# One visit of the divided array per chunk in a fused attention and feed-forward kernel

## The chip, the cores and the metric

The kernel runs on one core of a Trainium2 chip. The time is device microseconds (us) of that core for one execution. Five engines work side by side, each through its own list of instructions in order: TensorE (PE in the profile; its weight loads are PEld), VectorE (DVE), ScalarE (ACT), GpSimd (POOL) and SyncE (SP), which issues the transfers. They meet only through semaphores.

## The reference

Four batches, eight heads, 768 positions, 64 elements a head. Each query sees the 31 keys around it and, besides, 24 summaries of its head: the maximum of the keys and the mean of the values over blocks of 32. The attention's output, 3072 tokens of 512, goes through a feed-forward block with a squared relu.

```python
k_sum = k.reshape(B, H, nb, 32, D).max(axis=3)
v_sum = v.reshape(B, H, nb, 32, D).mean(axis=3)
scores_l = scale * q @ k.T                     # kept where abs(i - j) < 16
scores_s = scale * einsum('bhsd,bhnd->bhsn', q, k_sum) + log(32)
a = softmax(concatenate([scores_l masked, scores_s]))
x = a @ concatenate([v, v_sum])                # to (3072, 512)
r = maximum(x @ w_in, 0)                       # 512 -> 2048
out = (s * r * r + b) @ w_out                  # 2048 -> 512
```

Everything is float32.

## The kernel before

**Chunks, units and blocks.** The 3072 tokens are worked in twelve chunks `c` of 256 tokens, three to a batch. A chunk's attention is four units `p`, each one pair of heads. A unit has four stretches of 64 queries, and each stretch sees a window of 96 keys and the 24 summaries, 120 columns (`KR`). Its feed-forward part is sixteen blocks `f` of 128 hidden elements.

**A unit's way.** `load_unit` brings queries and key windows (tile `qk`), and `load_values` the value windows (`vw`). `fill_k` (L250) and `fill_v` (L255) copy the summaries into both, on POOL from chunk 2 on. `scores` (L285) multiplies 64x64 pieces: two heads and two stretches of queries use the four quarters of the array. `masked` (L306, DVE) adds the mask, scales, and finds the row's extreme. `exps` (L319, ACT) makes exponentials and sums, and `normalize` (L326 to L329, DVE) divides. `transposes` (L342, PE) turns the probabilities into a bank (`pt`), and `turned` (L349, ACT) copies them out (`pT`). `values` (L367) multiplies them by the value windows, in two halves of 64 columns of the array. From chunk 2 on two units share one output bank (`pav`), and `attended` (L377 on ACT, L379 on DVE) splits it into a rounded part `xh` and a rest `xl`, for both units at once.

**A block's way.** From chunk 1 on a product of float32 matrices is three products of rounded parts. `hidden` (L396) does twelve matmuls a block, two blocks to a bank (`ph`, two banks). `activate` does relu and square on ACT (L403, L404), scale and shift on POOL (`g`, L414), and the split into `gh` and `gl` on DVE (L416, L418), each in eight buffers. `project` (L433) does six matmuls a block into two banks (`po`), and `evict` (L441) copies these out after the sixteenth block.

**The order.** The whole order of work is written out as a plan. `at(step, order, fn, ...)` puts a piece of work at a step; step `16 * c + f` belongs to block `f` of chunk `c`. Steps run in order, within a step by the class (`LOAD, SPLIT, ATT, WEIGHTS, HID, PE_ATT, CHAIN, PROJ, EVICT`), within a class as entered. Every engine gets its instructions in this one order. From chunk 3 on the blocks go by fours: `hidden` of four blocks at steps 0, 4, 8 and 12 of a chunk (48 matmuls), their `activate` at their own steps in class `CHAIN`, and `project` of four blocks at steps 3, 7, 11 and 15 (24 matmuls), three steps and one hidden stretch behind: blocks 8 to 11 are projected at step 15.

A unit's attention is placed around the plan by `base`, the step of its scores, and nine `lags`. From chunk 4's third unit on (`by_fours`) units 0 and 1 of chunk `c` have their scores at step 14 of chunk `c - 2`, and units 2 and 3 eight steps later, at step 6 of chunk `c - 1`; values follow eight steps after the scores. So at each of these two steps PE does the values of two units and the scores of two others in one go, a **visit** of the divided array, before it returns to full 128x128 matmuls. Between visits stand two groups of transposes, at steps 3 and 11.

```python
base, v_at = NF * (c - 1) - 2 + 8 * (p // 2), 3 * (p % 2)
if by_fours(c, p):
    lags = (1, 1, 1, 2, 6, 5, 6, 8, 9)
m, e0, e1, n, fv, tr, tu, va, xa = (base + lag for lag in lags)
```

**Banks.** The eight banks of PSUM are two for `po`, two for `ph`, two for scores (`ps_s`, one a head, units 2k and 2k + 1 side by side), one for `pt` (`ps_t`) and one for `pav` (`ps_v`), which also takes the odd units' transposes.

**SP's queue.** It holds every transfer in the plan's order: `qk` and `vw` of each unit, the keys and values of a batch for the summaries (`load_k`, `load_v`, in four `stage` buffers that the output tiles of `evict` share), the small copies of `v_mean`, and the output's stores.

Of the kernel before, what the change touches and what calls it, by code (L numbers as in the profile page):

```python
# [10 lines left out]
F32 = mybir.dt.float32  # L11
F32R = mybir.dt.float32r
# [6 lines left out]
P = 128  # L19
# [7 lines left out]
KR = WIN + NB  # L27
NSUB = 4
T = NSUB * SUB
# [5 lines left out]
NF = DFF // P  # L35
# [9 lines left out]
def windowed_attention_then_relu2_ffn(ctx, tc, qk, vwin, kt, vt, kq, vrow, wp, sb, out):  # L45
# [8 lines left out]
    p2 = ctx.enter_context(tc.tile_pool(name="p2", bufs=2))  # L54
# [36 lines left out]
    def at(step, order, fn, *args):  # L91
        plan[step].append((order, len(plan[step]), fn, args))
# [167 lines left out]
    def scores_of_maxima(p):  # L260
        q, _ = qk_t[0, p]
        for i in range(NSUB):
            for e in range(2):
                r = slice(64 * e, 64 * e + 64)
                o = ps_of[0, p][e][64 * (i % 2) : 64 * (i % 2) + 64, i // 2]
                nc.tensor.matmul(o[:, WIN:], q[r, i * SUB : (i + 1) * SUB], ksum[0, p][r], start=True, stop=True)

    def scores(c, p, j):
        q, kw = qk_t[c, p]
        if j == 0:  # L270
            if c == 0 and p % 2:
                both = [ps_h.tile([P, 2, T], F32, name="ps", tag="ph") for _ in range(2)]
                ps_of[c, p] = [t[:, 0, : 2 * KR].rearrange("p (j k) -> p j k", k=KR) for t in both]
            elif c < 2:
                ps_of[c, p] = [ps_s.tile([P, 4, KR], F32, name="ps", tag="ps") for _ in range(2)]
            elif p % 2 == 0:
                both = [ps_s.tile([P, 4, KR], F32, name="ps", tag="ps") for _ in range(2)]
                ps_of[c, p], ps_of[c, p + 1] = [t[:, :2] for t in both], [t[:, 2:] for t in both]
        for e in range(2):
            r = slice(64 * e, 64 * e + 64)  # L280
            for a in range(2):
                i = 2 * j + a
                o, qi = ps_of[c, p][e][64 * a : 64 * a + 64, j], q[r, i * SUB : (i + 1) * SUB]
                if c > 1:
                    nc.tensor.matmul(o, qi, kw[r, i, :], start=True, stop=True)  # L285
                    continue
                w = win_start(i)
                near = kraw[0, p][r, w : w + WIN] if c == 0 else kw[r, i, :WIN]
                nc.tensor.matmul(o[:, :WIN], qi, near, start=True, stop=True)
                if c == 1:  # L290
                    nc.tensor.matmul(o[:, WIN:], qi, ksum[0, p][r], start=True, stop=True)

    def masked(c, p, j):
        _, ci = place(c)
        if j == 0 and c == 0:
            t = stage.tile([P, 4 * KR + 8], F32, name="pr0", tag="stage")
            pr_of[c, p] = t[:, : 4 * KR].rearrange("p (n k) -> p n k", k=KR)
            mn_of[c, p], sm_of[c, p] = t[:, 4 * KR : 4 * KR + 4], t[:, 4 * KR + 4 :]
        elif j == 0:
            t = p2.tile([P, 4 * KR + 16], F32, name="pr")  # L300
            pr_of[c, p] = t[:, : 4 * KR].rearrange("p (n k) -> p n k", k=KR)
            mn_of[c, p] = p2.tile([P, 4], F32, name="mn")
            sm_of[c, p] = p2.tile([P, 4], F32, name="sums")
        for e in range(2):
            n = 2 * e + j
            nc.vector.tensor_tensor_reduce(  # L306
                out=pr_of[c, p][:, n, :], in0=ps_of[c, p][e][:, j, :], in1=mask_of(NSUB * ci + 2 * j),
                scale=-1.0 / math.sqrt(D), scalar=3.0e38, op0=ALU.add, op1=ALU.min,
                accum_out=mn_of[c, p][:, n : n + 1],
            )  # L310
        if j == 1:
            ps_of.pop((c, p))
            qk_t.pop((c, p))
# [14 lines left out]
        pr = pr_of[c, p]  # L328
        nc.vector.tensor_tensor(pr, pr, rs.unsqueeze(2).to_broadcast([P, 4, KR]), ALU.mult)  # L329

    def by_fours(c, p):

        return (c, p) > (4, 1)

    def transposes(c, p):
        pr = pr_of.pop((c, p))
        if by_fours(c, p) and p % 2:
            pt_of[c, p] = ps_v.tile([P, 4 * P], F32, name="pt", tag="pav")
        else:
            pt_of[c, p] = ps_t.tile([P, 4 * P], F32, name="pt")  # L340
        for n in range(4):
            nc.tensor.transpose(pt_of[c, p][:KR, n * P : (n + 1) * P], pr[:, n, :], ident)  # L342

    def turned(c, p):
        if c == 0 and p > 1:
            pT_of[c, p] = slots.tile([KR, 4 * P], F32, name="pT0", tag="slot")
        else:
            pT_of[c, p] = p2.tile([KR, 4 * P], F32, name="pT")
        nc.scalar.copy(pT_of[c, p], pt_of.pop((c, p))[:KR])  # L349

    def values(c, p):
        vw, pT = vw_t.pop((c, p)), pT_of.pop((c, p))
        if c == 0 and p % 2:
            o_of[c, p] = ps_po.tile([P, DM], F32, name="pav", tag="po")
        elif c < 2 or p % 2 == 0:
            o_of[c, p] = ps_v.tile([P, 2 * T], F32, name="pav")
            if c > 1:
                o_of[c, p + 1] = o_of[c, p][:, T:]
        o = o_of[c, p]
        for i in range(NSUB):  # L360
            for e in range(2):
                oi, pi = o[64 * e : 64 * e + 64, i * SUB : (i + 1) * SUB], pT[:, e * T + i * SUB : e * T + (i + 1) * SUB]
                if c == 1:
                    nc.tensor.matmul(oi, vw[0:WIN, e, i, :], pi[0:WIN], start=True, stop=False)
                    nc.tensor.matmul(oi, vsum[0][0:KR, 2 * p + e], pi, start=False, stop=True)
                else:
                    nc.tensor.matmul(oi, vw[:, e, i, :], pi, start=True, stop=True)  # L367
# [32 lines left out]
    def activate(c, f):  # L400
        ph = ph_of.pop((c, f))
        r = p2.tile([P, T], F32, name="r")
        nc.scalar.activation(r, ph, AF.Relu)  # L403
        nc.scalar.activation(r, r, AF.Square)  # L404
        if c == 0:
            g = p2.tile([P, T], F32, name="g0", tag="gh", bufs=8)
            if f < 1:
                nc.vector.tensor_scalar(g, r, s_col, b_col, ALU.mult, ALU.add)
            else:
                nc.scalar.activation(g, r, AF.Identity, bias=b_col, scale=s_col)  # L410
            gg[c, f] = (g,)
            return
        g = p2.tile([P, T], F32, name="g")
        nc.gpsimd.tensor_scalar(g, r, s_col, b_col, ALU.mult, ALU.add)  # L414
        gh = p2.tile([P, T], F32R, name="gh", tag="gh", bufs=8)
        nc.vector.tensor_copy(gh, g)  # L416
        gl = p2.tile([P, T], F32R, name="gl", bufs=8)
        nc.vector.tensor_tensor(gl, g, gh.bitcast(F32), ALU.subtract)  # L418
        gg[c, f] = gh, gl

# [23 lines left out]
            nc.sync.dma_start(out[r0 : r0 + P, :], o)  # L444


    LOAD, SPLIT, ATT, WEIGHTS, HID, PE_ATT, CHAIN, PROJ, EVICT = range(9)


    FIRST, FIRST_SCALED, FIRST_TURNED = -100, 8, 2  # L450
# [31 lines left out]
    for c in range(1, NC):  # L482
        bi, ci = place(c)
        for p in range(NPAIR):
            if c == 1:

                base, v_at = [0,3,6,8][p], 0
                lags = (1, 2, 2, 3, 4, 4, 5, 6, 7)
            else:

                base, v_at = NF * (c - 1) - 2 + 8 * (p // 2), 3 * (p % 2)
                lags = ((1, 2, 2, 3, 6, 4, 5, 8, 9), (2, 3, 4, 5, 6, 6, 7, 8, 9))[p % 2]
                if by_fours(c, p):
                    lags = (1, 1, 1, 2, 6, 5, 6, 8, 9)
            m, e0, e1, n, fv, tr, tu, va, xa = (base + lag for lag in lags)
            if ci == 0:
                at(base - 7, LOAD, load_k, bi, p)
                at(base - 2, ATT, k_max, bi, p)
                if p < 2:
                    for third in range(3):  # L500
                        at(base + v_at - 5 + third, LOAD, load_v, bi, p, third)
                        at(base + v_at - 1 + third // 2, ATT, v_sum, bi, p, third)
                    at(base + v_at + 1, ATT, v_mean, bi, p)
            if (c, p) not in ((1, 0),):
                at(base - 6, LOAD, load_unit, c, p)
            at(base + v_at, LOAD, load_values, c, p)
            if c > 1:
                at(base - (2 if by_fours(c, p) else 1), ATT, fill_k, c, p)
            for j in range(2):
                at(base, PE_ATT, scores, c, p, j)  # L510
                at(m, ATT, masked, c, p, j)
                at((e0, e1)[j], ATT, exps, c, p, j)
            at(n, ATT, normalize, c, p)
            if c > 1:
                at(fv, ATT, fill_v, c, p)
            at(tr, PE_ATT, transposes, c, p)
            at(*((tr, CHAIN) if by_fours(c, p) else (tu, ATT)), turned, c, p)
            at(va, PE_ATT, values, c, p)
            if c < 2 or p % 2 == 0:
                at(xa, ATT, attended, c, p)  # L520
    for f in range(NF):
# [9 lines left out]
    for i in range(NC * NF):  # L531
        c, f = divmod(i, NF)
# [67 lines left out]
```

## Time and profile before

| | |
|---|---|
| time, median of 3 runs | 646.78 us (646.62 to 647.96) |
| the profiled execution, its own time | 646.86 us |
| its span, first to last instruction | 645.2 us |
| PE busy | 634.1 us, 98% |
| DVE, ACT, POOL busy | 332.4, 333.5, 155.6 us |

The span is that of the one profiled execution. Busy time of PE is modelled at the ends of matmuls, so it says little on how well the array is used. In a row of a timeline the columns are the start and the duration in us, the engine, the line of the kernel, the operation, output and inputs, shapes, and a count where instructions of one kind are drawn together; brackets at the end give idle time ahead of it and what ended it. The chain of work that ended last gives start, duration, engine, tile, line and count.

### The profile page before, as it was taken

The numbers are of one execution on the slowest core, as the hardware profiler recorded it, in microseconds if no ns is written. First come the engines' busy times: TensorE is split into PE (matmuls) and PEld (weight loads), VectorE is DVE, ScalarE is ACT, GpSimd is POOL, SyncE is SP. The second block draws the span as 40 slices with busy tenths as digits, with TensorE's granted clock in tenths as the row PEclk, the third lists the DMA queues.
The fourth block names the chain that finished last, engine by engine and source line by source line (L and its number), as shares of the span: only waits on it lengthen the run. The fifth ranks groups of instructions, "written<-read, shape, count | busy, mean of one in ns | idle before, by whom it ended". The sixth has DMA issues, their size and how long they took to land.

```text
span 645.2 us, 14148 instructions
## 1 busy us (share of the span) xinstructions
PE 634.1 (98%) x5316; PEld 554.8 (86%) x5316; DVE 332.4 (52%) x1076; ACT 333.5 (52%) x987; POOL 155.6 (24%) x325
## 2 busy tenths in 40 slices
PE   8799999999999999999999999999999999999997
PEld 6566668999989889989988998998899899899896
DVE  6897968885443533565433434347435334332311
ACT  5899997844445543534535434435535435443321
POOL 3000004143133223223233132131332232321211
PEclk9899999999999999999999999999999999999999
DMA  9999505045203202433400500513600500100000
GB/s 320 377 383 350 154 1 187 2 105 189 73 2 105 73 2 63 124 102 108 157 2 1 177 2 1 186 34 100 233 2 2 175 3 1 58 2 1 34 2 33
DMA packets 25606, 63.26 MB, mean 98 GB/s; under 512 B 3969, under 2 KB 3969, under 8 KB 25537
## 3 DMA queue, kind: packets, MB, share of 16 engines
q1 hardware_dynamic: 25536, 62.36, 29.3%
q8 instruction: 42, 0.69, 0.5%
q14 instruction: 28, 0.22, 0.1%
HBM read 55.90 MB, written 6.29 MB: 96 GB/s over the span
## 4 chain that ended last, share of the span: by engine, by line
PE 86%; ACT 8%; DMA 4%; SPq 0%; issue 0%
PE po L433 39%; PE ph L396 38%; PE pav L367 3%; PE ps L285 3%; DMA wraw<-in_wp_dram 3%; PE pt L342 3%; ACT wraw L118 2%; ACT wraw L119 2%; DMA vn<-in_vrow_dram 2%; ACT g L410 1%; ACT pr L319 1%; ACT r L404 1%; ACT r L403 1%; SPq L231 0%; ACT pT L349 0%
## 5 line engine op out<-in xcount | busy, mean ns | idle before, releaser
L414 POOL TENSOR_SCALAR g<-r,sb_col 128x256 f32<-128x256 f32 x176 | 102.2, 581 | 406.2 <-ACT r L404 349.5
L416 DVE CAST gh<-g 128x256 fp32r<-128x256 f32 x176 | 52.5, 298 | 274.1 <-POOL g L414 256.0
L403 ACT ACTIVATE r<-ph 128x256 f32<-128x256 f32 x192 | 72.3, 377 | 214.9 <-PE ph L396 214.9
L433 PE MATMUL po<-wh,gl 128*128 128x512 f32 x352 | 141.7, 402 | 0.0
L433 PE MATMUL po<-wh,gh 128*128 128x512 f32 x352 | 138.5, 393 | 0.0
L433 PE MATMUL po<-wl_out,gh 128*128 128x512 f32 x352 | 137.5, 391 | 0.0
L396 PE MATMUL ph<-xh,wl_in 128*128 128x256 f32 x704 | 110.3, 279 | 0.0
L396 PE MATMUL ph<-xl,wh 128*128 128x256 f32 x704 | 108.6, 276 | 0.0
L396 PE MATMUL ph<-xh,wh 128*128 128x256 f32 x704 | 108.6, 276 | 0.0
L396 PEld LDWEIGHTS ph<-xh,wl_in 128*128 128x128 f32 x704 | 97.1, 188 | 5.1 <-ACT r L404 0.5
L396 PEld LDWEIGHTS ph<-xl,wh 128*128 128x128 f32 x704 | 93.4, 188 | 0.0
L396 PEld LDWEIGHTS ph<-xh,wh 128*128 128x128 f32 x704 | 92.9, 188 | 0.0
L418 DVE TENSOR_TENSOR gl<-g,gh 128x256 fp32r<-128x256 f32 x176 | 85.1, 483 | 6.0
L404 ACT ACTIVATE r<-r 128x256 f32<-128x256 f32 x192 | 80.2, 418 | 6.1
L319 ACT ACTIVATE pr<-pr,mn 128x120 f32<-128x120 f32 x176 | 67.2, 383 | 24.7 <-DVE mn L306 24.7
L433 PEld LDWEIGHTS po<-wh,gl 128*128 128x128 f32 x352 | 66.1, 188 | 15.2 <-issue 1.6
L433 PEld LDWEIGHTS po<-wh,gh 128*128 128x128 f32 x352 | 66.1, 188 | 14.2
L433 PEld LDWEIGHTS po<-wl_out,gh 128*128 128x128 f32 x352 | 66.2, 188 | 13.0
L255 POOL COPY vw<-vsum 24x256 f32<-24x256 f32 x80 | 37.5, 509 | 1.3
L396 PEld LDWEIGHTS ph<-x,wf_in 128*128 128x128 f32 x128 | 25.7, 204 | 12.0 <-ACT r L403 3.4
L396 PE MATMUL ph<-x,wf_in 128*128 128x256 f32 x128 | 33.2, 406 | 1.6 <-ACT r L403 1.0
L329 DVE TENSOR_TENSOR pr<-pr,rs 128x480 f32<-128x480 f32 x48 | 32.3, 672 | 1.7
(82 smaller groups left out, 619.9 us busy)
## 6 DMA issues: line engine op xcount, KB each, us to landing
wraw<-in_wp_dram SPq DMA_DIRECT2D x32, 512.0 KB, 9.8
qk<-in_qk_dram SPq DMA_DIRECT2D x44, 368.0 KB, 4.6
vw<-in_vwin_dram SPq DMA_DIRECT2D x48, 192.0 KB, 6.5
out_dram<-o SPq DMA_DIRECT2D x24, 256.0 KB, 2.1
kraw<-in_kt_dram SPq DMA_DIRECT2D x12, 384.0 KB, 4.5
vraw<-in_vt_dram SPq DMA_DIRECT2D x12, 252.0 KB, 3.7
kq<-in_kq_dram SPq DMA_DIRECT2D x4, 512.0 KB, 4.1
vraw<-in_vt_dram SPq DMA_DIRECT2D x6, 264.0 KB
```

Source lines behind the costliest of these rows:

```text
L255: filler(c).tensor_copy(vw_t[c, p][WIN:KR, e], vsum[bi][WIN : WIN + NB, 2 * p + e, :].unsqueeze(1).to_broadcast([NB, NSUB, D]),)
L285: nc.tensor.matmul(o, qi, kw[r, i, :], start=True, stop=True)
L319: nc.scalar.activation(pr, pr, AF.Exp, bias=mn_of[c, p][:, n : n + 1], scale=-1.0, accum_out=sm_of[c, p][:, n : n + 1])
L329: nc.vector.tensor_tensor(pr, pr, rs.unsqueeze(2).to_broadcast([P, 4, KR]), ALU.mult)
L342: nc.tensor.transpose(pt_of[c, p][:KR, n * P : (n + 1) * P], pr[:, n, :], ident)
L396: nc.tensor.matmul(ph, w[:, kc * P : (kc + 1) * P], x[:, kc], start=(n == 0), stop=(n == len(terms) - 1))
L403: nc.scalar.activation(r, ph, AF.Relu)
L404: nc.scalar.activation(r, r, AF.Square)
L414: nc.gpsimd.tensor_scalar(g, r, s_col, b_col, ALU.mult, ALU.add)
L416: nc.vector.tensor_copy(gh, g)
L418: nc.vector.tensor_tensor(gl, g, gh.bitcast(F32), ALU.subtract)
L433: nc.tensor.matmul(po[t], a[:, t * P : (t + 1) * P], w, start=(f == 0 and n == 0), stop=(f == NF - 1 and n == len(terms) - 1),)
```

## The change

From chunk 4 on (`together(c)`, in place of `by_fours`) all four units of a chunk have the same `base`, step 15 of chunk `c - 2`. At that step PE does `values` of all four units of chunk `c - 1` and then `scores` of all four units of chunk `c`, in a new class `VISIT` behind `CHAIN` and ahead of `PROJ`. Chunk 4's scores join the values of the last two units of chunk 3, which stand one step ahead of them. Transposes of units 0 and 1 move to step 7 and those of 2 and 3 stay at step 11; between them and the visit are four steps or more.

Scores of units 2 and 3 go to the two `ph` banks, and their values to the bank of `pt`. Units 2 and 3 are masked and exponentiated first (`ATT`), units 0 and 1 behind them (`NEXT`), all in the step after the visit and ahead of that step's hidden blocks. `pr`, `mn`, `sums` and `pT` get four buffers in place of two, and `gl` seven in place of eight. Loads, fills and reductions move to steps that fit.

```diff
+    def together(c):
+        return c >= 4
     def scores(c, p, j):
...
+            elif p == 2 and together(c):
+                both = [ps_h.tile([P, 2 * T], F32, name="ps", tag="ph")[:, : 4 * KR] for _ in range(2)]
+                both = [t.rearrange("p (n k) -> p n k", k=KR) for t in both]
+                ps_of[c, p], ps_of[c, p + 1] = [t[:, :2] for t in both], [t[:, 2:] for t in both]
...
-            t = p2.tile([P, 4 * KR + 16], F32, name="pr")
+            t = p2.tile([P, 4 * KR + 16], F32, name="pr", bufs=4)
...
-            mn_of[c, p] = p2.tile([P, 4], F32, name="mn")
-            sm_of[c, p] = p2.tile([P, 4], F32, name="sums")
+            mn_of[c, p] = p2.tile([P, 4], F32, name="mn", bufs=4)
+            sm_of[c, p] = p2.tile([P, 4], F32, name="sums", bufs=4)
...
-        if by_fours(c, p) and p % 2:
+        if together(c) and p % 2:
             pt_of[c, p] = ps_v.tile([P, 4 * P], F32, name="pt", tag="pav")
...
-            pT_of[c, p] = p2.tile([KR, 4 * P], F32, name="pT")
+            pT_of[c, p] = p2.tile([KR, 4 * P], F32, name="pT", bufs=4)
...
-            o_of[c, p] = ps_v.tile([P, 2 * T], F32, name="pav")
+            if together(c) and p:
+                o_of[c, p] = ps_t.tile([P, 2 * T], F32, name="pav", tag="pt")
+            else:
+                o_of[c, p] = ps_v.tile([P, 2 * T], F32, name="pav")
...
-        gl = p2.tile([P, T], F32R, name="gl", bufs=8)
+        gl = p2.tile([P, T], F32R, name="gl", bufs=7)
...
-    LOAD, SPLIT, ATT, WEIGHTS, HID, PE_ATT, CHAIN, PROJ, EVICT = range(9)
+    LOAD, SPLIT, ATT, NEXT, WEIGHTS, HID, PE_ATT, CHAIN, VISIT, PROJ, EVICT = range(11)
...
-                if by_fours(c, p):
-                    lags = (1, 1, 1, 2, 6, 5, 6, 8, 9)
+                if together(c):
+                    base, v_at = NF * (c - 1) - 1, (9, 10, 4, 5)[p]
+                    tr = 8 + 4 * (p // 2)
+                    lags = (1, 1, 1, 2, (12, 13, 11, 11)[p], tr, tr, 16, 17)
...
-                at(base - 7, LOAD, load_k, bi, p)
-                at(base - 2, ATT, k_max, bi, p)
+                at(base - (12 - p if together(c) else 7), LOAD, load_k, bi, p)
+                at(base - (7 - p if together(c) else 2), ATT, k_max, bi, p)
...
-                at(base - (2 if by_fours(c, p) else 1), ATT, fill_k, c, p)
+                at(base - (2 if together(c) else 1), ATT, fill_k, c, p)
...
-                at(base, PE_ATT, scores, c, p, j)
-                at(m, ATT, masked, c, p, j)
-                at((e0, e1)[j], ATT, exps, c, p, j)
+                at(base, VISIT if together(c) else PE_ATT, scores, c, p, j)
+                at(m, NEXT if together(c) and p < 2 else ATT, masked, c, p, j)
+                at((e0, e1)[j], NEXT if together(c) and p < 2 else ATT, exps, c, p, j)
...
-            at(*((tr, CHAIN) if by_fours(c, p) else (tu, ATT)), turned, c, p)
-            at(va, PE_ATT, values, c, p)
+            at(*((tr, CHAIN) if together(c) else (tu, ATT)), turned, c, p)
+            at(va, VISIT if together(c) else PE_ATT, values, c, p)
```

More of the change, by code (lines that the diff above doesn't have):

```diff
@@ L329, in normalize @@
         nc.vector.tensor_tensor(pr, pr, rs.unsqueeze(2).to_broadcast([P, 4, KR]), ALU.mult)
-    def by_fours(c, p):
-        return (c, p) > (4, 1)
     def transposes(c, p):
         pr = pr_of.pop((c, p))
-        if by_fours(c, p) and p % 2:
+        if together(c) and p % 2:
             pt_of[c, p] = ps_v.tile([P, 4 * P], F32, name="pt", tag="pav")
```

## The prediction

> **What bounds the kernel now.** I read the page's shares first, then the chain that ended last.
>
> ```profile
> span 645.2 us, 14148 instructions
> PE 634.1 (98%) x5316; PEld 554.8 (86%) x5316; DVE 332.4 (52%) x1076; ACT 333.5 (52%) x987; POOL 155.6 (24%) x325
> ...
> PE 86%; ACT 8%; DMA 4%; SPq 0%; issue 0%
> PE po L433 39%; PE ph L396 38%; PE pav L367 3%; PE ps L285 3%; DMA wraw<-in_wp_dram 3%; PE pt L342 3%; ACT wraw L118 2%; ACT wraw L119 2%; DMA vn<-in_vrow_dram 2%; ACT g L410 1%; ACT pr L319 1%; ACT r L404 1%; ACT r L403 1%; SPq L231 0%; ACT pT L349 0%
> ```
>
> TensorE (PE) is busy 98% of the span, and the chain is PE's for 86% of it. The rest belongs to the opening (weights arriving, `wraw` and `vn`, and chunk 0's `g` at L410), which the change does not touch. After it the time is the sum of PE's work, and only what PE does or waits for counts. The chain in order of time shows the first visit that counts here, an irregular one, one half of a chunk, and the last visit:
>
> ```profile
> 189.35 1.08 PE pav L367 x32
> ...
> 208.94 0.61 PE pav L367 x16
> 209.55 0.11 issue
> 209.66 0.69 PE pav L367 x16
> ...
> 409.82 1.08 PE pav L367 x32
> 410.90 0.98 PE ps L285 x32
> 411.88 5.70 PE po L433 x24
> 417.58 5.47 PE ph L396 x48
> 423.05 0.87 PE pt L342 x8
> 423.92 5.50 PE po L433 x24
> 429.42 5.46 PE ph L396 x48
> 434.88 1.08 PE pav L367 x32
> ...
> 585.33 1.08 PE pav L367 x32
> ```
>
> A visit of the divided array is here 32 instructions of values (`pav`) and 32 of scores (`ps`). From one to the next are 25.06 us (409.82 to 434.88). The first projection stretch (`po`) after a visit takes 5.70 us, and the same 24 matmuls after transposes take 5.50, so leaving costs 0.20. How much of the visit itself is entering and switching, and how much is work, needs PE's own starts. Columns are start, us, and the count of instructions running in the window asked for:
>
> ```profile
> 409.75 0.28 PE L367 MATMUL pav<-pT,vw 120*64 120x64 f32 x2
> ...
> 409.86 0.40 PE L367 MATMUL pav<-pT,vw 120*64 120x64 f32 x8
> ...
> 410.62 0.29 PE L367 MATMUL pav<-pT,vw 120*64 120x64 f32 x4
> 410.83 0.33 PE L285 MATMUL ps<-qk 64*64 64x120 f32 x4
> ...
> 410.99 0.49 PE L285 MATMUL ps<-qk 64*64 64x120 f32 x12
> ...
> 411.50 0.39 PE L285 MATMUL ps<-qk 64*64 64x120 f32 x8
> ...
> 411.81 0.50 PE L433 MATMUL po<-wh,gl 128*128 128x512 f32 x1
> ```
>
> Values start in pairs and scores in fours. The second pair starts at 409.86 and the fifteenth of sixteen at 410.62 (its row holds the last four instructions), so 13 steps take 0.76 us, 0.0585 each. The second four of scores starts at 410.99 and the seventh of eight at 411.50: five steps, 0.102 each.
>
> **The change part by part.**
>
> *Fewer visits.* The instructions stay, and only their grouping changes. Before, from the visit with chunk 4's first scores to the last values, there are 17 visits (from 189.35 to 585.33 in the chain; one in 25 us, and one at 208.94, 20 us after the first). After, there are 9: chunk 4's scores with the last values of chunk 3, seven with four units of values and four of scores, and the values of chunk 11. Eight visits go. Work in a visit is 16 x 0.0585 = 0.936 and 8 x 0.102 = 0.816. What is not work is 1.08 - 0.94 = 0.14 on entering, 0.98 - 0.82 = 0.16 between values and scores, and 0.20 on leaving: 0.50 in all. Eight times that is 4.0 us. The bounds: if only the leaving belongs to the switch and the other 0.30 is paid for every eight matmuls' change of unit or bank, the gain is 1.6. At most every irregularity at a visit goes, 4.0 + 0.33 (next). I take 4.0, because the starts inside a visit are even and the extra sits at its three edges.
>
> The Trainium skill's "TensorEngine Tiling (Array Packing)", section Key Properties, says that changing the tiling mode, though not the tile, drains TensorE. By that rule both the change from full array to values and the one from values to scores are paid per visit, which gives the same 4.0, and the 1.6 would be wrong.
>
> *The irregular visit.* At 208.94 values take 0.61 + 0.11 + 0.69 = 1.41 instead of 1.08. The copy that they wait for follows its transposes directly there:
>
> ```profile
> 208.97 0.58 ACT L349 COPY pT<-pt 120x512 f32<-120x512 f32 x1 [2.28 <-PE pt L342]
> ```
>
> After the change chunk 4's transposes stand at steps 55 and 59 and its values at 63, so 0.33 us is won.
>
> *Scores of units 2 and 3 in the hidden banks (`ph`).* They now need both banks that the four hidden blocks just before them filled, so they wait for ScalarE's (ACT's) last relu. And the next hidden stretch waits until VectorE (DVE) has masked these scores.
>
> ```profile
> 407.20 0.38 ACT L403 ACTIVATE r<-ph 128x256 f32<-128x256 f32 x1 [2.21 <-PE ph L396]
> ...
> 407.94 0.36 ACT L403 ACTIVATE r<-ph 128x256 f32<-128x256 f32 x1
> ...
> 409.92 0.38 ACT L403 ACTIVATE r<-ph 128x256 f32<-128x256 f32 x1 [1.17 <-PE ph L396]
> ...
> 190.96 0.39 ACT L403 ACTIVATE r<-ph 128x256 f32<-128x256 f32 x1
> ```
>
> Count from V, a visit's first matmul (409.75 here). Block 14's relu starts at V + 0.17, block 15's 0.74 later (407.20 to 407.94), and it ends at V + 1.3. Units 2 and 3 are scored after 32 pairs of values (1.08 + 0.94) and units 0 and 1 (0.98): V + 3.0. So 1.7 us is spare. At the first merged visit, V = 189.28, the values are only 16 pairs, and the relu that counts is behind the attention copy: it starts at 190.96 and ends at V + 2.1, against scores due at V + 2.0. That costs 0.1 to 0.3, and I take 0.2.
>
> The other wait is the tight one. DVE's rows:
>
> ```profile
> 411.82 0.43 DVE L418 TENSOR_TENSOR gl<-g,gh 128x256 fp32r<-128x256 f32 x1
> 412.17 0.68 DVE L379 TENSOR_TENSOR xl<-pav,xh 128x512 fp32r<-128x512 f32 x1
> 412.77 0.27 DVE L306 CUSTOM_DVE_ANT_0 pr<-ps,mask_mid 128x120 f32<-128x120 f32 x1
> ...
> 412.97 0.28 DVE L306 CUSTOM_DVE_ANT_0 pr<-ps,mask_mid 128x120 f32<-128x120 f32 x1
> ```
>
> From start to start: `gl` 0.35, `xl` 0.60, one mask 0.20. With seven `gl` buffers instead of eight, `gl` of block 15 needs block 8 projected, and that comes right after the visit. Behind it on DVE stand both `xl` and the masks, so all of them wait too. The merged visit lasts 2.06 + 0.94 + 0.82 = 3.8; six projection matmuls are a quarter of 5.70, 1.4, and the last one's own run is 0.4. `gl` may start at V + 5.6 and is done by 6.0; two `xl` end at 7.2; eight masks at 8.8. The hidden stretch is due at V + 3.8 + 5.6 = 9.4 (5.70 less the 0.1 by which a matmul starts before the one ahead has ended). So 0.6 is spare, or 1.1 if the buffer is free after the fourth matmul, which is the last to read `gl`. I take a cost of 0. Without that cover each microsecond that the masks are late costs 8.
>
> *Softmax in one go.* Sixteen exps stand before the next relu on ACT instead of eight, and four normalizations instead of two before the next `gh`/`gl` on DVE.
>
> ```profile
> 413.48 0.38 ACT L319 ACTIVATE pr<-pr,mn 128x120 f32<-128x120 f32 x1
> ...
> 413.86 0.38 ACT L319 ACTIVATE pr<-pr,mn 128x120 f32<-128x120 f32 x1
> ```
>
> Sixteen take 6.1 us from about V + 7.4, so relu of block 0 starts at V + 13.5. Its bank is needed again by the second hidden stretch, at V + 9.4 + 5.5 + 5.5 = 20.4; four blocks' relus and squares end by V + 16.5. Normalization (1.0 us a unit by starts 418.36 and 419.35 below) ends near V + 20, and the first transposes stand after that stretch, at V + 25.9. Both are covered by projection stretches of 5.5.
>
> ```profile
> 418.36 0.16 DVE L326 TENSOR_SCALAR rs<-sums 128x4 f32<-128x4 f32 x1
> ...
> 419.35 0.16 DVE L326 TENSOR_SCALAR rs<-sums 128x4 f32<-128x4 f32 x1
> ```
>
> *Moved loads and fills.* SP now issues four `qk` loads together; their buffers are free after the visit, but the output stores stand ahead of them, behind the projection that ends at V + 20.4 and two copies. The fills need them at step 13, some 25 us later. Even one after another, at 4.6 us from issue to landing, they take 18:
>
> ```profile
> qk<-in_qk_dram SPq DMA_DIRECT2D x44, 368.0 KB, 4.6
> ```
>
> Where a batch starts, two value fills wait for small transfers behind these. If they hold GpSimd (POOL) at step 10 for one such landing, 4.6 us, `g` of blocks 10 and 11 queues behind them; these are projected two stretches (11 us) later. Four K fills stand ahead of `g` of block 13, at 0.26 to 0.28 each:
>
> ```profile
> L414 POOL TENSOR_SCALAR g<-r,sb_col 128x256 f32<-128x256 f32 x176 | 102.2, 581 | 406.2 <-ACT r L404 349.5 <-PE po L433 14.8 <-issue 12.6
> ...
> L250 POOL COPY qk<-ksum 128x96 f32<-128x96 f32 x40 | 10.3, 277 | 67.9 <-DMA qk<-in_qk_dram 62.6 <-DVE ksum L161 2.6 <-DVE wf_out L132 1.0
> ```
>
> Block 12's relu starts at V - 2.55 (407.20), relu and square take 0.74, its `g` 0.58, and four fills 1.1: they are done at V - 0.1, and the scores read them from V + 2.0. The batch starts' k and v loads move some steps earlier and stop SP at a buffer until DVE reduces the tile before, but the `k_max` and `v_sum` that wait stand two to four steps on. More buffers for probabilities and turned probabilities, and values of units 2 and 3 in the transposes' bank (last copied four steps before), add no instruction. All of this: 0.
>
> The sum: 646.86 (the profiled execution: 645.2 of span and 1.7 around it) - 4.0 - 0.33 + 0.2 = 642.7. That execution lies 0.08 above the median of the three runs shown, 646.78, so I give **642.7** for the median too.
>
> **The rivals.**
>
> *The hidden stretch waits for its banks* (slower). Place: the first hidden stretch of each chunk from 4 on. If the buffer of `gl` is counted free only with the last of the four projected blocks, `gl` of block 15 starts at V + 9.5, masks end at V + 12.7, and the stretch is 3.3 us late: 8 x 3.3 - 4.1 = +22, 669. From 0.6 to 1.1 us of delay on DVE or ACT on it costs something; 0.5 us more and it eats the gain. For it: the margin is small and three engines are in series. Against it: each block is projected by its own six matmuls, so a release after the sixth is all that my sum assumes.
>
> *Only the leaving is saved.* The gain is 1.6 + 0.1: 645.1. For it: the profile has no visit of more than 64 instructions, so I have not seen unit follow unit within values in two banks. Against it: the starts are even where unit follows unit now.
>
> *A longer burst is fed too slowly* (slower). If instructions 65 to 128 came at a hidden matmul's pace (5.47 / 48 = 0.114) instead of 1.75 / 64 = 0.027, a chunk would lose 5.6 and win 0.5: 646.8 + 8 x 5.1 = 687. It costs more than it wins from 8 ns per instruction. Against it: from the first to the last pair and four the pace does not fall, though PE uses 128 instructions, loads included, in 2 us.
> The Trainium skill's "TensorE: Matmul & The Clock Gate" names a queue 64 deep, and in "Wait — 56ns, not 53.3ns?" about 62 ns per matmul where the sequencer decodes. By that, 32 matmuls would come from the queue and 96 at 62 ns, an estimate of 6 us for a merged visit and some 660 in all; but here the scores, instructions 33 to 64 of a visit, already run at 0.102 / 4 = 26 ns, so the trace speaks against it.
>
> *The grouping isn't reached*: another matmul falls between values and scores. Then 17 visits stay, at 646.8. The order of work has none: within step 15 of a chunk values of the old and scores of the new chunk stand together.
>
> **How the numbers follow.** Forecast 0.75, only the leaving 0.10, banks late 0.08, slow feed 0.03, not reached or eaten by small waits 0.04. A measurement of this kernel tells some 0.2% from no change, that is 645.5 and 648.1. Late banks may also cost little: 0.01 of their 0.08 is still faster and 0.01 the same. So faster has 0.75 + 0.10 + 0.01 = 0.86, same 0.04 + 0.01 = 0.05, and slower 0.06 + 0.03 = 0.09. The forecast's own range is 641.8 (both edges of the sum at their best, with a few tenths of jitter) to 643.5. With the rival of 1.6 us it reaches to 645.4, which leaves out about 0.15.
>
> **What would show it.** In the changed profile the chain from 212 us on should have one visit in 49.7 us, with values x64 at 2.0 and scores x64 at 1.8, the projection after it at 5.7, and none at the place of the other. `gl` on DVE should wait about 2.5 us for PE once a chunk. If hidden matmuls wait for DVE at a chunk's start, the margin was wrong; if scores wait for ACT within the visit, the relu was late. Visits much longer than 4.0 us would make the even pace wrong.

## The result and the profile after

The changed kernel takes 642.35 us (median of six runs, 642.22 to 643.41), the kernel before in the same comparison 646.96 (646.51 to 647.96). The ratio is 0.993, with a 95% interval of 0.9917 to 0.9943. Faster was forecast, at 642.7.

The page's shares, and the chain that ended last, of the kernel after. In the changed file L374 are values, L293 scores, L440 projections, L403 hidden matmuls and L346 transposes.

```profile
span 640.6 us, 14293 instructions
PE 629.6 (98%) x5316; PEld 552.3 (86%) x5316; DVE 328.8 (51%) x1076; ACT 330.6 (52%) x987; POOL 164.2 (26%) x325
```

```profile
189.11 1.08 PE pav L374 x32
190.19 2.01 PE ps L293 x64
192.20 2.96 PE po L440 x12
...
232.52 2.02 PE pav L374 x64
234.53 1.80 PE ps L293 x64
236.34 5.70 PE po L440 x24
242.03 5.47 PE ph L403 x48
247.50 5.49 PE po L440 x24
252.99 5.47 PE ph L403 x48
258.46 0.87 PE pt L346 x8
259.34 5.50 PE po L440 x24
...
282.14 2.02 PE pav L374 x64
```

PE is as full as before and still sets the time; the same 5316 matmuls only stand in other groups. A chunk, from one visit to the next, takes 49.62 us (232.52 to 282.14), where two halves of 25.06 stood. Twice the values take 2.02 and not 2.16, and twice the scores 1.80 and not 1.96. The projection of 5.70 comes once a chunk, and where the other visit stood the projection takes 5.49 (247.50). The first merged visit shows 2.01 for its scores, 0.21 more than the later ones.

The opening, which the change does not touch, moves by itself: the first visit here starts at 189.11, in the profile before at 189.35, and in the experiments that have this visit between 188.7 and 190.3. So the stretch from that visit to the span's end is the better measure of what PE does, and I call it the tail: 645.2 - 189.35 = 455.8 before, 640.6 - 189.11 = 451.5 after, 4.3 less.

The wait that the prediction called tight, on VectorE (columns as in the prediction's timelines) at the last visit shown. Its first matmul, V, starts at 282.07 on PE, 0.07 ahead of the row in the chain, which counts from the end of the matmul before. PE's row first, then VectorE's:

```profile
282.07 0.28 PE L374 MATMUL pav<-pT,vw 120*64 120x64 f32 x2
```

```profile
284.84 0.28 DVE L423 CAST gh<-g 128x256 fp32r<-128x256 f32 x1
287.12 0.42 DVE L425 TENSOR_TENSOR gl<-g,gh 128x256 fp32r<-128x256 f32 x1 [2.00 <-PE po L440]
287.47 1.28 DVE L386 TENSOR_TENSOR xl<-pav,xh 128x512 fp32r<-128x512 f32 x2
288.66 0.27 DVE L314 CUSTOM_DVE_ANT_0 pr<-ps,mask_first 128x120 f32<-128x120 f32 x1
...
290.08 0.28 DVE L314 CUSTOM_DVE_ANT_0 pr<-ps,mask_mid 128x120 f32<-128x120 f32 x1
```

The hidden stretch that waits for these masks, from PE's timeline:

```profile
291.51 0.63 PE L403 MATMUL ph<-xh,wl_in 128*128 128x256 f32 x4
```

`gl` of block 15 waits 2.00 us for the projection and starts at V + 5.05. The eight masks that free the two banks end at 290.36. The hidden stretch starts at 291.51, so 1.15 us is spare. Over the kernel this wait is long, and no matmul feels it:

```profile
DVE gl L425 <- PE po L440: 14.0, 8, 2.0
```

### The profile page after: what moved, and what is told of

It reads as the page before. It is cut to its first block, busy times and chain, and to the rows that moved or that the text cites. A ratio compares the mean times of both kernels' runs of the same rounds, so it can differ in the third digit from the quotient of the medians.

```text
span 640.6 us, 14293 instructions
## 1 busy us (share of the span) xinstructions
PE 629.6 (98%) x5316; PEld 552.3 (86%) x5316; DVE 328.8 (51%) x1076; ACT 330.6 (52%) x987; POOL 164.2 (26%) x325
## 4 chain that ended last, share of the span: by engine, by line
PE 88%; ACT 9%; DMA 2%; DVE 1%; issue 0%; DVEq 0%
PE po L440 39%; PE ph L403 38%; PE pav L374 4%; PE pt L346 3%; PE ps L293 3%; ACT wraw L118 2%; ACT wraw L119 2%; DMA wraw<-in_wp_dram 2%; ACT pr L327 1%; ACT g L417 1%; ACT r L411 1%; PE warm L202 1%; ACT r L410 1%; DVE pr L314 0%; ACT pT L353 0%
## 5 line engine op out<-in xcount | busy, mean ns | idle before, releaser
L421 POOL TENSOR_SCALAR g<-r,sb_col 128x256 f32<-128x256 f32 x176 | 109.0, 620 | 387.6 <-ACT r L411 283.9
L440 PE MATMUL po<-wh,gl 128*128 128x512 f32 x352 | 141.1, 401 | 0.0
L440 PE MATMUL po<-wh,gh 128*128 128x512 f32 x352 | 138.5, 393 | 0.0
L440 PE MATMUL po<-wl_out,gh 128*128 128x512 f32 x352 | 137.4, 390 | 0.0
L403 PE MATMUL ph<-xh,wl_in 128*128 128x256 f32 x704 | 110.2, 279 | 0.0
L403 PE MATMUL ph<-xl,wh 128*128 128x256 f32 x704 | 108.6, 276 | 0.0
L403 PE MATMUL ph<-xh,wh 128*128 128x256 f32 x704 | 108.6, 276 | 0.0
L403 PEld LDWEIGHTS ph<-xh,wl_in 128*128 128x128 f32 x704 | 97.2, 188 | 5.2 <-ACT r L411 0.5
L425 DVE TENSOR_TENSOR gl<-g,gh 128x256 fp32r<-128x256 f32 x176 | 81.9, 465 | 29.9 <-PE po L440 14.0
L403 PEld LDWEIGHTS ph<-xl,wh 128*128 128x128 f32 x704 | 93.4, 188 | 0.0
L403 PEld LDWEIGHTS ph<-xh,wh 128*128 128x128 f32 x704 | 92.9, 188 | 0.0
L440 PEld LDWEIGHTS po<-wh,gh 128*128 128x128 f32 x352 | 66.1, 188 | 14.4
L440 PEld LDWEIGHTS po<-wh,gl 128*128 128x128 f32 x352 | 66.2, 188 | 13.9 <-issue 1.6
L440 PEld LDWEIGHTS po<-wl_out,gh 128*128 128x128 f32 x352 | 66.2, 188 | 13.0
L403 PEld LDWEIGHTS ph<-x,wf_in 128*128 128x128 f32 x128 | 24.6, 198 | 13.0 <-ACT r L410 5.1
L403 PE MATMUL ph<-x,wf_in 128*128 128x256 f32 x128 | 32.7, 401 | 1.7 <-ACT r L410 1.0
L448 ACT COPY o<-po 128x512 f32<-128x512 f32 x24 | 14.0, 585 | 38.9 <-PE po L440 36.3
```

What stands on the lines that cost most here:

```text
L403: nc.tensor.matmul(ph, w[:, kc * P : (kc + 1) * P], x[:, kc], start=(n == 0), stop=(n == len(terms) - 1))
L440: nc.tensor.matmul(po[t], a[:, t * P : (t + 1) * P], w, start=(f == 0 and n == 0), stop=(f == NF - 1 and n == len(terms) - 1),)
```

## The experiments

The theory: a visit pays a fixed price at its edges, about 0.50 us, and the gain is eight of these; all new waits are covered, the hidden stretch's wait for its banks by 1.15 us. The rivals: only leaving is paid per visit; the gain comes from the moved work and not from the count; the covers are not what they seem.

**The price of a visit by itself.** An extra visit with no use is put into each of the eight chunks, between the first hidden stretch and the projection behind it, once with two and once with eight rounds of fours.

```diff
+    def extra_visit(n):
+        t = ps_s.tile([P, 4, KR], F32, name="extra", tag="ps")
+        u = ps_s.tile([P, 4, KR], F32, name="extra", tag="ps")
+        for k in range(n):
+            for e, o in enumerate((t, u)):
+                r = slice(64 * e, 64 * e + 64)
+                for a in range(2):
+                    nc.tensor.matmul(
+                        o[64 * a : 64 * a + 64, k % 4], ones[r, :SUB], ones[r, :KR], start=True, stop=True
+                    )
...
+        if c >= 4 and f == 3:
+            at(i, VISIT, extra_visit, 2)        # and extra_visit, 8
```

> The changed kernel with one extra visit in each of the eight chunks from 4 on, between the first hidden stretch and the projection behind it: 8 matmuls of ones in 64x64 quarters (16 instructions, four fours) into the score banks, whose output nobody reads. Theory: each costs its work, 4 x 0.102 = 0.41, and entering and leaving, 0.34: 8 x 0.75 = 6.0, 648.4 us. Rival (only leaving costs): 8 x 0.61 = 4.9, 647.2.

> The same extra visits with 32 matmuls (64 instructions, sixteen fours). Theory: 16 x 0.102 = 1.63 of work and the same 0.34: 8 x 1.97 = 15.8, 658.1 us; the difference to the smaller extra visit is 12 x 0.102 = 1.22 a visit, so what is left at zero instructions is the price of the edges. Rival (only leaving costs): 8 x 1.83 = 14.6, 657.0. Rival (a longer burst is fed more slowly): the sixteen fours take clearly more than 1.63.

They took 648.18 and 658.53 us, one execution each. The chain of the small and of the large one:

```profile
241.64 5.47 PE ph L415 x48
247.11 0.57 PE extra L309 x16
247.68 5.70 PE po L452 x24
```

```profile
242.19 5.47 PE ph L415 x48
247.66 1.80 PE extra L309 x64
249.46 5.71 PE po L452 x24
```

Sixteen instructions take 0.57 and 64 take 1.80: twelve more fours cost 1.23, 0.1025 each. At no instruction 0.57 - 0.41 = 0.16 is left, and the projection behind it is 0.21 longer than the 5.49 of one that follows hidden matmuls. So a visit with scores alone pays 0.37, 0.03 more than expected. The whole span agrees: the tails are 6.25 and 16.05 us longer than the changed kernel's, 0.78 and 2.01 for each of the eight visits. The rival's 0.20 is little more than half of it. The large one also shows that 64 instructions in one mode keep the pace of the first sixteen.

**The grouping undone, all else kept.** Units 0 and 1 have their values and scores first, then come one or two projected blocks, then units 2 and 3.

```diff
-    ... CHAIN, VISIT, PROJ, EVICT = range(11)
+    ... CHAIN, VISIT, FIRST_PROJ, SECOND_VISIT, PROJ, EVICT = range(13)
...
-                at(base, VISIT if together(c) else PE_ATT, scores, c, p, j)
+                at(base, (VISIT if p < 2 else SECOND_VISIT) if together(c) else PE_ATT, scores, c, p, j)
...
-            at(va, VISIT if together(c) else PE_ATT, values, c, p)
+            at(va, (VISIT if p < 2 else SECOND_VISIT) if together(c) else PE_ATT, values, c, p)
...
-        at(done, PROJ, project, c, f)
+        at(done, FIRST_PROJ if c > 2 and f == 8 else PROJ, project, c, f)      # then: f in (8, 9)
```

> The changed kernel with the grouping alone undone: at step 15 values and scores of units 0 and 1, then the six projection matmuls of block 8, then values and scores of units 2 and 3, then blocks 9 to 11. Buffers, banks, loads and the order on the other engines stay. Theory (each visit pays about 0.50 us at its edges: entering 0.14, values to scores 0.16, leaving 0.20): seven more visits, 642.35 + 3.5 = 645.9 us. Rival (only leaving is paid per visit, 0.20): 642.35 + 1.4 = 643.8. Rival (the gain came from the moved work and buffers, not from the count of visits): 642.4.

> As the kernel with the grouping alone undone, but with blocks 8 and 9 (twelve projection matmuls) between the two visits in place of block 8 alone. There the extra visit cost 0.52 us a chunk on PE as the theory says (3.6 of the 6.6 that its span grew), and 2.7 more came from fourteen hidden stretches in which each matmul followed the last by 118 ns in place of 114. Theory (the 118 ns are a matter of how the matmuls fall behind the visit, not of the visits' count): 645.9 us if the pace returns to 114, up to 649 if it does not; the visits themselves cost 7 x 0.52 more than merged ones in either case. Rival (two visits a chunk with the new banks slow the hidden stretches by themselves): 118 ns again in the same fourteen stretches, 649.

Both took 649.5 us (648.92 to 650.1 and 649.09 to 650.06), ratios to the kernel before of 1.0034 (1.002 to 1.0048) and 1.004 (1.0025 to 1.0055). That is 7.15 more than the changed kernel and twice the 3.5 that I had expected. The chain of the first shows what is in it:

```profile
238.06 4.33 PE po L440 x18
242.39 5.65 PE ph L403 x48
248.05 5.51 PE po L440 x24
253.56 5.66 PE ph L403 x48
259.21 0.87 PE pt L346 x8
```

Visit and projections together take 9.94 us by their starts, against 2.01 + 1.80 + 5.61 = 9.42 in the changed kernel: 0.52 a chunk, 3.6 in all, as the theory says. The rest is new: the next two hidden stretches take 5.65 and 5.66, not 5.47 and 5.46. In fourteen such stretches each matmul follows the last by 118 ns, not by 114, which makes 2.7. No wait stands in them. In the last chunk, whose visit has values alone, the division costs 0.38; my 3.5 had left this eighth visit out. Together these are 6.7 of the 6.8 by which the tail grows. With twelve projection matmuls between the visits instead of six, which I thought might mend the pace, the same fourteen stretches are slow and both tails are 458.3 us. So the visits' price is as predicted, and a second price that I had not foreseen is paid by this arrangement; its cause is open (last section).

**Half of the change.** `together(c)` is true from chunk 8 on, and chunks 4 to 7 keep the lags of before. Further lines give these chunks their old fills, bank for transposes and class of `turned`.

```diff
     def together(c):
-        return c >= 4
+        return c >= 8
+    def by_fours(c, p):
+        return (c, p) > (4, 1) and c < 8
...
```

> The change applied only from chunk 8 on; chunks 4 to 7 as before the change. 13 visits in place of 17. Theory (gain follows the count of visits): half the gain, 4 x 0.50 = 2.0, less 0.2 for the first merged visit's wait, and chunk 4's irregular visit stays: 646.9 - 1.8 = 645.1 us. Rival (the gain is mostly something done once, as the irregular visit of chunk 4): 646.5 to 646.9.

It took 645.8 us (645.02 to 646.1), ratio 0.998 (0.997 to 0.9989): 0.7 to 1.9 us won by the interval, where 1.8 was forecast. Its tail is 454.4, 1.4 less than before. Four visits are gone, 2.0; the first merged visit again has scores of 2.01, 0.2 lost; and one group of transposes at 298.9, long before the first merged visit, waits 0.47 for VectorE by PE's starts, some 0.4 more than at this place in the kernel before. So the gain comes with the visits, not all at once in one place.

**The irregular visit of chunk 4**, in the kernel before:

```diff
     def by_fours(c, p):
-        return (c, p) > (4, 1)
+        return c > 3
```

> The kernel before, with units 0 and 1 of chunk 4 also placed by the lags that the later units have. Theory (0.33 us of the gain is chunk 4's irregular visit, whose copy follows its transposes directly): values there take 1.08 in place of 1.41, and the span falls by 0.33, 646.5 us. Rival: the wait has another cause and stays at 1.41.

One execution, 646.78 us. In its chain:

```profile
189.63 1.08 PE pav L367 x32
...
202.86 0.87 PE pt L342 x8
203.74 5.46 PE ph L396 x48
209.19 1.08 PE pav L367 x32
```

With the transposes one hidden stretch ahead, the values take 1.08, not 1.41, and the tail falls from 455.8 to 455.4. The time itself could not show this, since the opening came 0.3 later. The 0.33 in the sum is right.

**The cover of the banks.** Three kernels move the masks of units 2 and 3. In one they stand behind those of units 0 and 1; in the others `gl` has six or five buffers.

```diff
-                at(m, NEXT if together(c) and p < 2 else ATT, masked, c, p, j)
-                at((e0, e1)[j], NEXT if together(c) and p < 2 else ATT, exps, c, p, j)
+                at(m, NEXT if together(c) and p > 1 else ATT, masked, c, p, j)
+                at((e0, e1)[j], NEXT if together(c) and p > 1 else ATT, exps, c, p, j)
```

```diff
-        gl = p2.tile([P, T], F32R, name="gl", bufs=7)
+        gl = p2.tile([P, T], F32R, name="gl", bufs=6)      # and bufs=5
```

> Only the order of the softmax is changed: units 0 and 1 are masked and exponentiated before units 2 and 3, whose scores hold the banks of the hidden blocks. The masks that release these banks end eight masks later, 1.6 us. Theory (in the changed kernel the banks are free 1.15 us before the next hidden stretch, 0.35 at the first merged visit): hidden matmuls wait 0.4 us in seven chunks and 1.3 in the first, 642.35 + 4.1 = 646.5. Rival (the banks are not what the hidden stretch is near to waiting for): 642.4.

> Six buffers for gl in place of seven. Blocks 14 and 15 now wait for blocks 8 and 9 to be projected, so the masks end one block's projection later, 1.37 us, against 1.15 us that are spare. Theory: 0 to 0.2 us of wait in seven chunks, 642.4 to 643.8. Rival (the margin is larger, or the wait is not passed on through VectorE's order): 642.35, and no wait of hidden matmuls.

> Five buffers for gl. Block 15 waits for block 10 to be projected, 2.75 us later than in the changed kernel. Theory: the hidden stretch waits 2.75 - 1.15 = 1.6 us, less 0.2 because the first bank is free one mask earlier, in seven chunks: 10 to 11 us, 652.4 to 653.5. Rival (the wait is not passed on): 642.4.

The swapped masks took 648.31 us (647.41 to 648.85), ratio 1.0016 (1.0007 to 1.0026) to the kernel before: 6.0 above the changed kernel, where 4.1 was forecast; by the tails it is 456.6 - 451.5 = 5.1. Now PE waits for VectorE, and the chain runs through the masks:

```profile
PE ph L403 <- DVE mn L314: 2.9, 8, 1.1
```

```profile
237.87 1.15 PE po L440 x4
...
239.04 0.42 DVE gl L425
239.46 1.20 DVE xl L386 x2
...
243.49 0.20 DVE pr L314
...
243.84 5.70 PE ph L403 x48
```

The order that the prediction drew stands here as the chain: four projection matmuls free `gl`, then `gl`, both `xl`, the masks, and the hidden stretch. The row of waits counts idle time alone. By PE's starts a chunk loses 0.44 ahead of the stretch and 0.08 within it, and the first merged visit 1.6 in all. The 0.08 is no wait for the second bank, which is first written by the stretch's 25th matmul, and that comes at the usual pace: it stands between the first matmul and the second, 0.195 from start to start in place of 0.118. In a stretch that waited, the first weight load starts 0.03 ahead of its matmul, and in the changed kernel 0.24 ahead; whether this makes the 0.08 was not tested.

Six buffers took 645.02 us and five 655.65, one execution each. With six, PE's hidden stretch starts 0.18 late and loses 0.07 within, 7 x 0.25 = 1.75 of the 2.1 by which the tail grows, and one pair of stretches at the slow pace of 118 ns makes the rest; I had expected 0 to 0.2 for each. With five it starts 1.55 late in each of seven chunks, 10.9 of 12.1; for the rest, two such pairs account for some 0.8, and the 0.07 within again for 0.5. (The execution's time is 13.3 above the changed kernel's, since its opening is 1.2 later.) Here the chain goes the same way, and the last link is ACT's exps, which read the masks' result:

```profile
237.54 3.88 PE po L440 x16
...
241.44 0.42 DVE gl L425
241.86 1.20 DVE xl L386 x2
...
243.30 1.25 ACT pr L327 x6
...
244.62 5.69 PE ph L403 x48
```

So the cover is real, and behind it each microsecond is paid in every chunk. The three delays measure it: the masks come 1.64, 1.38 and 2.75 us later than in the changed kernel and the stretch 0.44, 0.18 and 1.55, so 1.20 is covered each time. The chain's last steps before PE are inferred. In the code an exp reads the masked copy and not the bank, so it can't hold the bank. And the stretch starts (244.62 with five buffers) after the seventh of the eight masks has ended (244.47) and before the eighth has (244.68): by the code the seventh is the last to read the first bank. In the changed kernel the stretch starts 1.35 after the seventh's end (290.16), here 0.15 after it, which gives the 1.20 again; the 1.15 above is counted from the eighth.

**The wait taken away.** `gl` has its eight buffers again, and the summed values one buffer instead of two.

```diff
-            vsum[bi] = p2.tile([P, H, D], F32, name="vsum")
+            vsum[bi] = p2.tile([P, H, D], F32, name="vsum", bufs=1)
...
-        gl = p2.tile([P, T], F32R, name="gl", bufs=7)
+        gl = p2.tile([P, T], F32R, name="gl", bufs=8)
```

> Eight buffers for gl as before the change, and one for the summed values in place of two, to make room. Theory (the wait of gl for the projection, 14.0 us over eight chunks on VectorE, is covered): the wait is gone, the masks end some 2 us earlier, and the time stays, 642.35 within 0.3. Rival (part of the wait reaches the hidden stretch): faster by up to 8 x 0.2 = 1.6, 640.8.

It took 642.15 us (641.88 to 642.51), ratio 0.9921 (0.9904 to 0.9937). VectorE no longer waits: in its timeline `gl` follows `gh`, and the first mask starts at V + 4.6 (V is 282.26 here), in the changed kernel at V + 6.6.

```profile
285.01 0.28 DVE L423 CAST gh<-g 128x256 fp32r<-128x256 f32 x1
285.32 0.42 DVE L425 TENSOR_TENSOR gl<-g,gh 128x256 fp32r<-128x256 f32 x1
285.67 1.28 DVE L386 TENSOR_TENSOR xl<-pav,xh 128x512 fp32r<-128x512 f32 x2
286.87 0.27 DVE L314 CUSTOM_DVE_ANT_0 pr<-ps,mask_first 128x120 f32<-128x120 f32 x1
```

The tail is the same as the changed kernel's to 0.1 us (640.8 - 189.2 against 640.6 - 189.1). The 14.0 us of wait cost nothing.

**The change taken further**, on top of the last: merged visits from chunk 3 on.

```diff
-        return c >= 4
+        return c >= 3
...
-        n = (1, 2, 2, 4)[min(c, 3)]
+        n = (1, 2, 4, 4)[min(c, 3)]
```

> The change taken further: merged visits from chunk 3 on, with hidden blocks by fours from chunk 2 on, eight buffers for gl and one for the summed values. One visit fewer than in the changed kernel. Theory (gain follows the count of visits, if the first merged visit's waits stay as they are): 642.35 - 0.5 = 641.8 us. Rival (chunk 1 and 2 still split weights on VectorE and ScalarE, so masks or relus are late there): 642.4 or more, with waits of hidden matmuls near 140 us.

It took 642.31 us (641.72 to 643.19), ratio 0.9931 (0.9918 to 0.9943): no different from the changed kernel. Its first merged visit starts at 139.57, and its span of 640.7 ends 501.1 us later; in the changed kernel the visit at that place starts at 138.82 and the end is 501.8 later. The chain of the one, and of the changed kernel:

```profile
139.57 1.08 PE pav L374 x32
140.65 2.01 PE ps L293 x64
```

```profile
138.82 1.08 PE pav L374 x32
139.90 0.98 PE ps L293 x32
```

So PE does win 0.7 from there on, but the opening was 0.75 later in the profiled execution. Of this, 0.65 stands already one visit earlier (114.25 against 113.60 by PE's starts), where the profiles of the other kernels lie between 113.2 and 114.8; the other 0.1 is mostly one hidden stretch at the slow pace (last section). Whether the 0.65 is chance or chunk 1 pays for it, five runs don't tell.

## Why the prediction was right

*The sum.* Forecast 642.7, measured 642.35. By the tails the change gave 4.3, where the sum had 4.0 + 0.33 - 0.2 = 4.13. The 0.17 between them was not foreseen: in the chain of the kernel before two groups of transposes, three chunks apart, take 0.95 in place of 0.87, and from the first merged visit on none does in the changed kernel.

```profile
297.67 0.95 PE pt L342 x8
...
448.11 0.95 PE pt L342 x8
```

The other 0.2 of the profiled span is the opening, 189.35 to 189.11; it arises before the visit at 113.6, from which on both kernels take the same 75.44 us to this one. Since the opening varies by 1.6 us between executions, that the medians meet the forecast to 0.35 is in part luck, and the 4.3 is the better test.

*Eight visits at 0.50.* A chunk went from 50.12 to 49.62, as the sum has it. The edges were also measured alone: 0.37 for a visit with scores only, 0.38 for one with values only, and 0.52 for a full one in the kernel with the grouping undone, so the passage from values to scores is about 0.15. The rival that only leaving is paid (645.1) falls with this. A change of number format alone is not the price either: by the code transposes are float32 like values and scores, but on the full array, and eight of them take 0.87 with a projection of 5.50 behind them, against 5.49 behind hidden matmuls.
The Trainium skill's "TensorEngine Tiling (Array Packing)", section Key Properties, has the array drained at a change of tiling mode; the trace agrees in that each such change is paid, with about 0.15 at each change into a smaller mode and 0.21 on the way back to the full array, but it does not show that the time is a drain.

*The irregular visit.* 0.33 forecast, values at 1.08 in place of 1.41 in the kernel before with only this mended.

*The first merged visit.* 0.2 forecast, 0.21 measured: scores of 2.01 against 1.80, with the relu starting at V + 1.68 behind the attention copy, as before.

*The tight wait.* I had 0.6 to 1.1 us spare, the latter if `gl` is free after the fourth projection matmul. It is: `gl` starts at V + 5.05 and not V + 5.6, and so waits 2.0 at most, where I had some 2.5; 1.15 is spare to the eighth mask, 1.2 by the delays. That rival's price per microsecond was right too: five buffers cost 1.55 a chunk. Where masks or `gl` were delayed on purpose, I had the wait itself (0.4 for 0.44 with the masks swapped, 1.4 to 1.6 for 1.55 with five buffers) but forecast too little in all: I left out the 0.07 to 0.08 after the first matmul of a stretch that waited, and the slow pace of some stretches.

*Softmax, loads and fills at 0.* The sixteen exps end and the relu of block 0 starts at V + 13.0 (V + 13.5 in the prediction), and in a full chunk no hidden stretch, and no projection stretch behind the same kind of work, differs from its length before by more than 0.02. GpSimd does wait at batch starts for the small transfers, 8.1 us in six waits of at most 3.5; nothing of it is in the chain that ended last.

```profile
295.06 0.36 ACT L410 ACTIVATE r<-ph 128x256 f32<-128x256 f32 x1
...
POOL vw L255 <- DMA vsum<-vmean: 8.1, 6, 3.5
```

*A longer burst.* 64 scores in 1.80 us are 28 ns each with the edge, like 32 in 0.98 (31 ns). The rival of slow feed falls.
By the 62 ns that the Trainium skill's "TensorE: Matmul & The Clock Gate" gives in "Wait — 56ns, not 53.3ns?" for decoding by the sequencer, these 64 alone would take 4.0 us by an estimate; no run here shows that pace.

## What to carry to other kernels

When one engine is full, count how often it changes its mode, not only what it does: here a visit of the divided array cost 0.37 to 0.38 us with one kind of matmul in it and 0.50 to 0.52 with two, however many there were, and the price could be read before the change from the starts at the edges of one visit. Grouping moves waits, so follow each bank and buffer that the grouped work now holds, queue by queue, to the next moment when PE needs it, and write down the spare time. A wait of 14 us on another engine may cost nothing, and the same wait 1.4 us longer per chunk is past its cover and costs.

## What was not expected

Hidden matmuls have two paces. Each stretch begins with some 118 ns from start to start; usually it falls to 113 or 114 after the first five, but in some stretches it stays at 118 to the end, 5.65 against 5.47 us. With two visits close together it stayed slow in the first two hidden stretches of seven chunks, whether six or twelve projection matmuls stood between the visits, and was gone after the next transposes. With five or six `gl` buffers it came in single chunks, in two stretches in a row; with the masks swapped and in the kernel that begins at chunk 3 in one stretch each. From 232 to 262 us VectorE and ScalarE are as busy in the slow case (15.7 and 16.8 us) as in the changed kernel (15.9 and 16.7), the granted clock is 1.00 in both, and no wait stands in these stretches. What sets the pace was not found, and no experiment here took it apart.

The opening of the program varies by 1.6 us between profiled executions, more than a third of what the change gives. The tail behind it repeated to 0.1 us where the work on PE was the same.
